# Loading the first dilated q and k in fp32 from SyncE, an earlier trigger for the casts of later batches, and shorter assumed latencies

## The chip, the cores and the metric

The kernel runs on one core of one Trainium2 chip. The metric is the device time of one execution in microseconds (us). Several executions of each kernel are timed, in rounds that alternate with runs of the kernel before on the same chip. A run counts as slow when it is over 1.5% above the fastest run of its own kernel; verdicts compare fast runs alone. A ratio is the mean time of one kernel's fast runs over that of the other's fast runs of the same rounds, so it is not quite the ratio of the medians quoted beside it. The interval in brackets is the 95% one.

In what follows PE is the TensorE, DVE the VectorE, ACT the ScalarE, POOL the GpSimd and SP the SyncE; "SPq" lines are SyncE's DMA issues. "L822" is a line of the kernel; lines of the changed kernel stand 10 or 11 below those of the kernel before (L811 there is L822 here).

## The reference, cut

```python
def attn(q, k, v):              # B, H, S, D = 8, 8, 576, 64
    scores = (1 / np.sqrt(D)) * np.matmul(q, k.transpose(0, 1, 3, 2))
    rel = pos[:, None] - pos[None, :]
    mask_plain = (rel >= 0) & (rel < 32)                        # heads 0 to 3
    mask_dil = (rel >= 0) & (rel < 128) & (rel % 4 == 0)        # heads 4 to 7
    ...                                                         # masked softmax
    return np.matmul(attn, v)

def moe(x, w_in, w_out, beta):  # x: 4608 tokens x 512, d_ff = 2048
    h = x @ w_in
    return (h * (1.0 / (1.0 + np.exp(-beta * h)))) @ w_out
```

All inputs are fp32. The output of the attention is `x`, token by token, for the feed-forward.

## The kernel before

The program isn't written in the order in which it runs. Every piece of work is an operation with its candidate engines, an assumed duration, the operations it depends on and a priority `vt`; a list scheduler simulates the engines and emits each instruction, to each engine's in-order stream, when the simulated engine is free. So an assumed latency changes no transfer. It changes where the instructions stand, and the hardware then keeps to that order.

The feed-forward runs in nine tiles of 512 tokens. A tile's 16 hidden blocks need `xT`, the transposed attention output. Batches 0 to 2 are loaded by GpSimd as a casting DMA and transposed by PE. From batch 3 on the way is longer:

```python
def back_dma(b, j, vt_of, vdone):            # attention output -> DRAM -> xT, for b >= 2, by SyncE
    ...                                      # spills of x; assumed: dma=1200, lat=2000
    o = plan.op([("SP", 1300)], lambda e: nc.sync.dma_start_transpose(out=cols, in_=rows[:]), out + dil,
                vt_of[f"X1{j}"], dma=1500, lat=3500)
...
def spread(e):                               # v of a batch into its padded place
    copy(e, vd[kv][:, :, :, 0:D], vd16_of[b])
o = plan.op([("POOL", 1100), ("DVE", 620)], spread, [ld["vd"][0], ...], vt, sbuf=True)
...
def t_pace(e, b=b, mid=mid):                 # what releases the casts of batch b >= 4
    nc.gpsimd.tensor_copy(out=pace[:], in_=xT[0:1, 0, mid - 1:mid + 1])
go = plan.op([("POOL", 150)], t_pace, behind + xready(mid - 1, mid + 1), b - 2.4)
for n, (z, h0) in enumerate(((0, 4), (1, 4), (0, 0), (1, 0))):
    c = cast(b, z, h0, [go], b - 2 + .01 * n)                 # GpSimd: fp32 -> bf16 scratch in DRAM
    ld[b]["x", z, h0] = crossbar(b, z, h0, [c] + ..., ...)    # SyncE: transposing load of the scratch
```

SyncE's one stream thus carries the transposes of k and q, the spills of x, the transposes of x and the stores of the output. A spill is the write of an attention output from the core's memory to DRAM.

The names in the traces: `dk` and `dq` are k and q of the dilated heads, `kT` and `qT` those of the plain heads; `pt` and `ptd` are the exponentials of the scores, plain and dilated; `vd` is v of the dilated heads; `g` is a hidden block after its gate; `s` is the scratch in DRAM that the casts write; `st` is a buffer for loads.

The softmax here doesn't subtract the row's maximum and nothing guards it: scores larger than these inputs give would overflow.

Of the kernel before, what the change touches and what calls it, by code (L numbers as in the profile page):

```python
# [174 lines left out]
def kernel(  # L175
# [55 lines left out]
    def copy(e, out, in_):  # L231
        (nc.scalar.copy if e == "ACT" else E[e].tensor_copy)(out=out, in_=in_)  # L232
# [12 lines left out]
    parity = const([P, 2], BF16, "parity")  # L245
    zero = const([P, 256], BF16, "zero")
    warm = const([P, 1], FP32, "warm")
    pace = const([1, 2], BF16, "pace")

    xT = const([P, NKT, B * S], BF16, "xT")  # L250
    g_t = [const([P, NFB, NTOK], BF16, f"g{i}") for i in range(2)]
# [129 lines left out]


    def dma(queue, out, in_):
        {"POOL": nc.gpsimd, "SP": nc.sync}[queue].dma_start(out=out, in_=in_)  # L384

    def load(queue, args, deps, vt, kb, rate=.4, issue=750, lat=1100):
        return plan.op(
# [3 lines left out]
    def direct_qk(b, z, h0, deps, vt):  # L391
        rows, n, dst = ((2 * GD, RD, std) if h0 else (P, RP, stp))
        src = bass.AP(tensor=(k, q)[z].tensor, offset=(k, q)[z][b, h0].offset,
                      ap=[[n * D, rows], [2 * S * D, 2], [1, n * D]])
        return load("POOL", (dst[z], src), deps, vt, 576, .41 if b else .33, lat=1100 if b else 1500)

    def plain_v(b, p0, c0):
        return bass.AP(tensor=v.tensor, offset=v[b, 0].offset + (p0 - WIN) * D + c0 * QT * D,
# [11 lines left out]
    def direct_vd(b, deps, vt, tdeps=()):  # L410
        src = v[b, 4:8].rearrange("h (t T) d -> t h (T d)", T=C)[0:P]
        out = [load("POOL", (vd16_of[b].rearrange("p h T d -> p h (T d)"), src), deps, vt, 512, .35)]
        for c in range(2):
            src = bass.AP(tensor=v.tensor, offset=v[b, 4].offset + ((P - WIN) * C + c) * D,
                          ap=[[2 * D, 2 * KTL], [S * D, 4], [1, D]])
            out.append(load("POOL", (vt_[b % 2][:, c, :, 0:D], src), list(tdeps), vt + (1.245 if b == 0 else .02 if b < DIRECT else 0) + .001 + .001 * c, 96, .2))
        return out

    scratch = {}
# [42 lines left out]
    def used(key, o):  # L462
        last.setdefault(key, []).append(o)
# [7 lines left out]
    def back_dma(b, j, vt_of, vdone):  # L471

        rows = dram_pool.tile([S // 2, HD], BF16, name=f"x{b}_{j}")
        out = [plan.op(
            [("SP", 500)], lambda e: nc.sync.dma_start(
                out=rows[:, 0:HD // 2].rearrange("(i m) c -> m i c", m=QT),
                in_=xsp[j][:].rearrange("p a x h d -> p a (x h d)")),
            [vdone[0, j], vdone[1, j]], vt_of[f"X1{j}"], dma=1200, lat=2000)]
        dep = [vdone[x, rp] for x in (2, 3) for rp in range(2)]
        t0, t1 = (0, S // 2 // C) if j == 0 else (S // 2 // C, P)  # L480
        right = rows[:, HD // 2:].rearrange("(t r) c -> t r c", r=C)
        dil = [plan.op(
            [("SP", 500)], lambda e: nc.sync.dma_start(
                out=right[0:t1 - t0], in_=xdm[t0:t1].rearrange("p r x h d -> p r (x h d)")),
            dep, vt_of["X2"] if j == 0 else vt_of["X11"], dma=1100, lat=2000)]
        if j:
            dil.append(plan.op(
                [("SP", 500)], lambda e: nc.sync.dma_start(
                    out=right[t1 - t0:].rearrange("u c e -> c u e"), in_=xdt[:].rearrange("p x h d -> p (x h d)")),
                [vdone["U"]], vt_of["X11"], dma=300, lat=2000))  # L490
        for x in range(2):
            wrote(("xs", x, j))
            for o in out:
                used(("xs", x, j), o)
        if j == 0:
            wrote("xdm", "xdt")
        for o in dil[:1]:
            used("xdm", o)
        for o in dil[1:]:
            used("xdt", o)  # L500
        cols = xT[:, :, b * S + j * S // 2:b * S + (j + 1) * S // 2]
        o = plan.op([("SP", 1300)], lambda e: nc.sync.dma_start_transpose(out=cols, in_=rows[:]), out + dil,
                    vt_of[f"X1{j}"], dma=1500, lat=3500)
        xcopy.append((range(NKT), b * S + j * S // 2, b * S + (j + 1) * S // 2, o))

    def attention(b, ld, names, vts):
# [4 lines left out]
        if b < DIRECT:  # L511
            for n in [x for x in names if x[0] in "KQ"]:
                z, kind, i = "KQ".index(n[0]), n[1], int(n[2])
                vt = vt_of[n]
                g = Group("a")
                src = ld["qk", z, 0 if kind == "P" else 4]
                tr = plan.op([("PE", (18 * mm(64) if kind == "P" else 6 * mm(QT)))],
                             lambda e, g=g, z=z, kind=kind, i=i: t_transposes(g, z, kind, i),
                             [src, ident], vt, acquire=g)
                used(("st", z), tr)  # L520
                def evac(e, g=g, z=z, kind=kind, i=i):
                    tp = bank(g, BF16)[:, 0:S]
                    if kind == "P":
                        dst = qT[kv][:, i] if z else kT[kv][:, i, WIN:]
                        copy(e, dst.rearrange("p (g j) -> p g j", j=RP), tp.rearrange("p (j g) -> p g j", j=RP))
                    else:
                        copy(e, (dk, dq)[z][kv][:, i].rearrange("p h (g s) -> p h g s", s=3),
                             tp.rearrange("p (s h g) -> p h g s", s=3, h=4))
                key = (("kT", "qT")[z], kv, i) if kind == "P" else (("dk", "dq")[z], kv, i)
                steps[n] = [plan.op([dve(S), act(S)], evac, [tr, fill1] + war(key), vt, group=g)]  # L530
                wrote(key)
        else:
            ready = {"D": [ld["x", 0, 4], ld["x", 1, 4]], "P": [ld["x", 0, 0], ld["x", 1, 0], fill1]}
# [262 lines left out]


    w_in_ld, w_out_ld = {}, {}
    gop, oread = {}, {}
    count = [0, 0]  # L800

    def slot_h(t, fb, c0, n, vt, apart):
# [37 lines left out]
    def block_cols(t, tb, vts, lo, hi, last_one):  # L840
        g = Group("z" if t == NTT - 1 else "o")
        prev = None
        for part in range(4):
            def mms(e, part=part):
                for fb in range(4 * part, 4 * part + 4):
                    nc.tensor.matmul(bank(g)[:, lo:hi], lhsT=g_t[t % 2][:, fb, tb * P:(tb + 1) * P],  # L846
                                     rhs=w_out_bf[:, fb, lo:hi], start=(fb == 0), stop=(fb == NFB - 1))
            deps = [prev] + [o for fb in range(4 * part, 4 * part + 4) for o in gop[t, fb]]
            prev = plan.op([("PE", 4 * mm(hi - lo))], mms, deps + [w_out_ld[part]], vts[part],
                           acquire=g if part == 0 else None, group=g)  # L850
        oread.setdefault(t, []).append(prev)
        ob = osb[count[1] % 4]
        key = ("osb", count[1] % 4)
        count[1] += 1
        r0 = t * NTOK + tb * P
        w = war(key)
        wrote(key)

        def evac(e):
            if e == "ACT":  # L860
                nc.scalar.mul(out=ob[:, lo:hi], in_=bank(g)[:, lo:hi], mul=0.5)  # L861
            else:
                nc.vector.tensor_single_scalar(out=ob[:, lo:hi], in_=bank(g)[:, lo:hi], scalar=0.5, op=ALU.mult)
        ev = plan.op([act(hi - lo), dve(hi - lo)], evac, [prev] + w, vts[3] - .01, group=g)
        so = plan.op([("ACT" if last_one and hi == HD else "SP", 400)],
                     lambda e: (nc.scalar if e == "ACT" else nc.sync).dma_start(out=out[r0:r0 + P, lo:hi], in_=ob[:, lo:hi]),
                     [ev], vts[3], dma=.5 * (hi - lo) * 1000 / 350)
        used(key, so)



    ld = {b: {} for b in range(B)}
    for n, (z, h0) in enumerate(((0, 4), (1, 4), (0, 0), (1, 0))):
        ld[0]["qk", z, h0] = direct_qk(0, z, h0, [], -9 + .01 * n)
    ld[0]["vd"] = direct_vd(0, [], -8.5, [fill3])
    ld[0]["vp"] = direct_vp(0, [fill3], -8.4)
    for n, (c0, c1) in enumerate(((0, 512), (512, 1024), (1024, 2048))):
# [21 lines left out]
    first = FIRST.split()  # L899
    names0 = first + ["zPRE", "zVAL"]  # L900
    vts = [-3 + 2 * i / len(first) for i in range(len(first))] + [-3, -2.5]
    vts[first.index("T"):len(first)] = [-.5, -.4, -.3, -.2]
    attention(0, ld[0], names0, vts)

    def xready(lo, hi, kts=range(NKT)):
# [2 lines left out]
    def loads(b):  # L908
# [7 lines left out]
            ld[b]["vp"] = direct_vp(b, war(("vp", b % 2)) + [fill4], base + .06)  # L916
            wrote(("vp", b % 2))
        else:
            behind = [ld[b - 1]["x", z, h0] for z in range(2) for h0 in (0, 4)] if b > DIRECT else []

            mid = (b - 2) * S + S // 2

            def t_pace(e, b=b, mid=mid):
                nc.gpsimd.tensor_copy(out=pace[:], in_=(  # L924
                    xT[0:1, 0, mid - 1:mid + 1] if b - 2 >= BY_DMA else g_t[b % 2][0:1, 0, 0:2]))
            go = plan.op([("POOL", 150)], t_pace, behind + (
                xready(mid - 1, mid + 1) if b - 2 >= BY_DMA else gop[b - 2, 0]), b - 2.4)
            for n, (z, h0) in enumerate(((0, 4), (1, 4), (0, 0), (1, 0))):
                c = cast(b, z, h0, [go], b - 2 + .01 * n)
                key = [(((("dk", "dq") if h0 else ("kT", "qT"))[z]), b % 2, i) for i in range(2)]  # L930
# [61 lines left out]
```

## Time and profile before

| | before |
|---|---|
| median of the runs beside the changed kernel | 305.85 us (305.43 to 306.01) |
| profiled span, granted clock | 304.8 us, 1.0 |
| PE busy | 295.4 us, 97% |
| PE waits over 0.25 us after 18 us | two: 0.26 (w_in) and 1.19 (dq) |

The prediction shows the lines for these. One view has to be added to it, the stream of SyncE (columns: start, length of the issue, what). It is that of the stretch which goes differently later:

```profile
81.77 2.70 SPq L502 DMA_TRANSPOSE xT<-x  x2
...
95.09 1.79 SPq L502 DMA_TRANSPOSE xT<-x  x1
97.07 4.55 SPq L438 DMA_TRANSPOSE dk<-s  x1
...
108.99 2.68 SPq L438 DMA_TRANSPOSE qT<-s  x1
```

The reader is to see the order: in 81 to 96 us three transposes of x, and only behind them the four transposes of batch 4's k and q, which wait for casts.

### The profile page before, as it was taken

How to read it: one execution, taken by the hardware profiler on the slowest of the kernel's cores; microseconds unless marked ns; L12 is line 12 of the kernel's file. 1: busy time of each engine (PE TensorE's matmuls, PEld its weight loads, DVE VectorE, ACT ScalarE, POOL GpSimd, SP SyncE). 2: the span in 40 equal slices, each digit the busy share in tenths (PEclk: the TensorE clock that was granted, in tenths of full speed). 3: DMA queues.
4: the chain of work that ended last, by engine and by line, in shares of the span. 5: the costliest groups of instructions: out<-in, count | busy, mean ns of one | idle time of the engine just before them, and what ended most of it. 6: DMA issues, size and time to landing. Idle time of an engine off the chain costs nothing.

```text
span 304.8 us, 6036 instructions
## 1 busy us (share of the span) xinstructions
PE 295.4 (97%) x2312; PEld 148.7 (49%) x2312; DVE 182.5 (60%) x422; ACT 171.0 (56%) x315; POOL 90.1 (30%) x132
## 2 busy tenths in 40 slices
PE   6899999999999989999999999999999999999995
PEld 5564545554544444444444444444444444444454
DVE  3468965888866745875677567757764434343300
ACT  2767963877547644755565556556554454554411
POOL 8978662746055104600470065100000000000000
PEclk9999999999999999999999999999999999999999
DMA  6999999999989998999699999992332100010122
GB/s 102 172 210 202 206 184 208 180 142 167 204 193 193 149 152 170 197 137 237 134 180 177 158 202 173 173 231 58 95 92 73 39 34 34 34 37 34 50 88 71
DMA packets 117376, 42.47 MB, mean 139 GB/s; under 512 B 93748, under 2 KB 110916, under 8 KB 117348
## 3 DMA queue, kind: packets, MB, share of 16 engines
q0 software_dynamic: 66672, 19.66, 64.9%
q1 hardware_dynamic: 50532, 22.36, 37.1%
q8 instruction: 18, 0.29, 0.4%
q14 instruction: 10, 0.08, 0.1%
q10 hardware_dynamic: 144, 0.07, 0.1%
HBM read 39.32 MB, written 18.87 MB: 191 GB/s over the span
## 4 chain that ended last, share of the span: by engine, by line
PE 74%; DMA 16%; POOL 3%; SPq 2%; DVE 2%; issue 1%; ACT 0%; POOLq 0%; DVEq 0%
PE bank L846 36%; PE bank L811 32%; DMA vd<-in_v_dram 4%; DMA st<-in_q_dram 4%; DMA dq<-s 3%; DMA w_in_bf<-in_moe_w_in_dram 3%; DMA x<-xsp 2%; DVE g L825 2%; SPq L438 2%; PE bank L673 1%; PE bank L729 1%; PE bank L639 1%; PE bank L714 1%; POOL st L384 1%; POOL vp L384 1%
## 5 line engine op out<-in xcount | busy, mean ns | idle before, releaser
L846 PE MATMUL bank<-w_out_bf,g 128*128 128x512 bf16 (+2 forms) x608 | 143.3, 368 | 0.0
L825 DVE SCALAR_TENSOR_TENSOR g<-tnh,bank 128x512 bf16<-128x512 bf16 x144 | 97.7, 685 | 74.4 <-ACT tnh L820 73.7
L811 PE MATMUL bank<-xT,w_in_bf 128*128 128x512 bf16 (+1 forms) x584 | 141.2, 376 | 0.3 <-DMA w_in_bf<-in_moe_w_in_dram 0.3
L820 ACT ACTIVATE tnh<-bank,beta_half 128x512 bf16<-128x512 f32 x144 | 98.5, 689 | 74.4 <-PE bank L811 73.3
L811 PEld LDWEIGHTS <-w_in_bf 128*128 128x128 bf16 x584 | 54.7, 98 | 60.4 <-DMA w_in_bf<-in_moe_w_in_dram 0.4
L846 PEld LDWEIGHTS <-g 128*128 128x128 bf16 x608 | 54.6, 98 | 55.7
L861 ACT ACTIVATE osb<-bank 128x512 f32<-128x512 f32 (+1 forms) x36 | 21.2, 589 | 32.0 <-PE bank L846 31.8
L576 ACT ACTIVATE pt<-bank 128x288 bf16<-128x288 f32 x64 | 21.5, 418 | 5.5 <-PE bank L673 5.4
L576 ACT ACTIVATE ptd<-bank 128x512 bf16<-128x512 f32 x32 | 16.9, 603 | 6.5 <-PE bank L639 6.5
L596 DVE TENSOR_TENSOR xsp<-bank,rcp 96x384 bf16<-96x384 f32 x32 | 17.7, 554 | 1.1
L384 POOL DMA_DIRECT2D vp<-in_v_dram x10 | 17.7, 1776 | 0.5 <-PE bank L455 0.5
L595 DVE RECIPROCAL rcp<-bank 128x4 f32<-128x4 f32 (+2 forms) x72 | 12.9, 180 | 6.3 <-PE bank L729 4.8
L580 DVE TENSOR_TENSOR ptd<-ptd,mask_d 128x512 bf16<-128x512 bf16 x27 | 11.9, 452 | 5.6 <-ACT ptd L576 4.5
L924 POOL COPY pace<-xT 1x2 bf16<-1x2 bf16 x4 | 0.8, 207 | 47.1 <-DMA xT<-x 37.1
L596 DVE TENSOR_TENSOR xdm<-bank,rcp 128x256 bf16<-128x256 f32 x32 | 13.6, 425 | 1.1
L384 POOL DMA_DIRECT2D vt<-in_v_dram x16 | 13.5, 1020 | 0.0
L384 POOL DMA_DIRECT2D s<-in_q_dram x10 | 13.5, 1347 | 0.0
L729 PEld LDWEIGHTS <-pt 128*128 128x128 bf16 x192 | 9.4, 97 | 5.9
L384 POOL DMA_DIRECT2D s<-in_k_dram x10 | 11.2, 1121 | 1.1 <-issue 1.1
L232 POOL COPY dkt<-dk 128x384 bf16<-128x384 bf16 x7 | 3.8, 544 | 22.8 <-DMA dk<-s 17.4
L729 PE MATMUL bank<-vp,pt 128*128 128x65 bf16 x192 | 10.4, 193 | 0.0
L714 PEld LDWEIGHTS <-ptd 128*128 128x128 bf16 x128 | 6.7, 98 | 4.7 <-issue 0.2
(108 smaller groups left out, 177.2 us busy)
## 6 DMA issues: line engine op xcount, KB each, us to landing
out_dram<-osb SPq DMA_DIRECT2D x35, 256.0 KB, 2.7
s<-in_k_dram POOLq DMA_DIRECT2D x10, 288.0 KB, 7.0
s<-in_q_dram POOLq DMA_DIRECT2D x10, 288.0 KB, 10.3
vp<-in_v_dram POOLq DMA_DIRECT2D x7, 384.0 KB, 18.2
w_out_bf<-in_moe_w_out_dram POOLq DMA_DIRECT2D x2, 1024.0 KB, 16.3
st<-in_k_dram POOLq DMA_DIRECT2D x6, 288.0 KB, 13.8
st<-in_q_dram POOLq DMA_DIRECT2D x6, 288.0 KB, 12.7
x<-xsp SPq DMA_DIRECT2D x12, 144.0 KB, 7.3
```

The costliest lines, as they stand in the source:

```text
L384: {"POOL": nc.gpsimd, "SP": nc.sync}[queue].dma_start(out=out, in_=in_)
L576: nc.scalar.activation(out=w(), in_=sc(), func=ACT.Exp, scale=SCALE)
L580: E[e].tensor_tensor(out=w(), in0=w(), in1=m(), op=ALU.mult)
L595: nc.vector.reciprocal(out=r, in_=p[..., D])
L596: nc.vector.tensor_tensor(out=dst, in0=p[..., 0:D], in1=r.unsqueeze(len(p.shape) - 1).to_broadcast(list(p.shape[:-1]) + [D]), op=ALU.mult)
L714: nc.tensor.matmul(pv[:, r, a], lhsT=ptd[:, x - 2, j, 2 * r + a], rhs=vd[kv][:, 2 * (x - 2) + a, 2 * r + j, 0:D + 1], start=True, stop=True)
L729: nc.tensor.matmul(pv[:, a, h2, :], lhsT=pt[x][:, (3 * j + a) * 2 + h2], rhs=vp[kv][:, (2 * x + h2) * NI + 3 * j + a, 0:D + 1], start=True ...
L811: nc.tensor.matmul(bank(g)[:, a:z], lhsT=w_in_bf[:, kt, fb * P:(fb + 1) * P], rhs=xT[:, kt, xo + a:xo + z], start=(i == 0 and kt == kts[0] ...
L820: nc.scalar.activation(out=th[:, 0:n], in_=bank(g)[:, 0:n], func=ACT.Tanh, scale=beta_half[:, fb:fb + 1])
L825: nc.vector.scalar_tensor_tensor(out=g_t[t % 2][:, fb, c0:c0 + n], in0=th[:, 0:n], scalar=1.0, in1=bank(g)[:, 0:n], op0=ALU.add, op1=ALU.mult)
L846: nc.tensor.matmul(bank(g)[:, lo:hi], lhsT=g_t[t % 2][:, fb, tb * P:(tb + 1) * P], rhs=w_out_bf[:, fb, lo:hi], start=(fb == 0), stop=(fb = ...
L861: nc.scalar.mul(out=ob[:, lo:hi], in_=bank(g)[:, lo:hi], mul=0.5)
```

## The change

The intent: start the first loads sooner by giving the dilated k and q of batch 0 to SyncE in fp32 (ACT and DVE then cast them); put the tail part of batch 0's attention into tile 0; release the casts of batch b at the first output block of tile b - 3, rather than when xT of batch b - 2 has landed; and tell the scheduler shorter latencies for the way of x back into xT. Cut to its core (left out: shorter assumed times for GpSimd's first loads, and bookkeeping):

```diff
+    def first_dil(z):
+        stage = g_t[1][...].bitcast(FP32)...
+        o = load("SP", (stage, src), [], -9.1 + .01 * z, 576, .41, 400, 300)
+        return [plan.op([("ACT", ...), ("DVE", ...)],
+                        lambda e, x=x: copy(e, std[z][:, x], stage[:, x]), [o], ...) for x in range(2)]
 ... spills of x
-            [vdone[0, j], vdone[1, j]], vt_of[f"X1{j}"], dma=1200, lat=2000)]
+            [vdone[0, j], vdone[1, j]], vt_of[f"X1{j}"], dma=900, lat=1300)]
 ... transpose of x
-                    vt_of[f"X1{j}"], dma=1500, lat=3500)
+                    vt_of[f"X1{j}"], dma=1400, lat=2200)
 ... batch 0
-        ld[0]["qk", z, h0] = direct_qk(0, z, h0, [], -9 + .01 * n)
+        ld[0]["qk", z, h0] = first_dil(z) if h0 else direct_qk(0, z, h0, [], -9 + .01 * n)
-    vts[first.index("T"):len(first)] = [-.5, -.4, -.3, -.2]
+    vts[first.index("T"):len(first)] = [.2,.35,.45,.5]
 ... trigger of the casts
-            behind = [ld[b - 1]["x", z, h0] for z in range(2) for h0 in (0, 4)] if b > DIRECT else []
-            go = plan.op([("POOL", 150)], t_pace, behind + xready(mid - 1, mid + 1) ..., b - 2.4)
+            ev, ob, key = evac_of[b - 3, 0] if b > DIRECT else (gop[b - 2, 0][-1], None, None)
+            go = plan.op([("POOL", 150)], t_pace, [ev], b - 2.4)       # copies one element of ob
```

More of the change, by code (lines that the diff above doesn't have):

```diff
@@ L247 @@
     warm = const([P, 1], FP32, "warm")
-    pace = const([1, 2], BF16, "pace")
+    pace = const([1, 1], FP32, "pace")
     xT = const([P, NKT, B * S], BF16, "xT")
@@ L383, in dma @@
     def dma(queue, out, in_):
-        {"POOL": nc.gpsimd, "SP": nc.sync}[queue].dma_start(out=out, in_=in_)
+        {"POOL": nc.gpsimd, "SP": nc.sync, "ACT": nc.scalar}[queue].dma_start(out=out, in_=in_)
     def load(queue, args, deps, vt, kb, rate=.4, issue=750, lat=1100):
@@ L394, in direct_qk @@
                       ap=[[n * D, rows], [2 * S * D, 2], [1, n * D]])
-        return load("POOL", (dst[z], src), deps, vt, 576, .41 if b else .33, lat=1100 if b else 1500)
+        return load("POOL", (dst[z], src), deps, vt, 576, .41, lat=1100 if b else 1300)
+    def first_dil(z):
+        stage = g_t[1][0:2 * GD, 8 * z:8 * z + 6, :].rearrange("p f n -> p (f n)").bitcast(FP32).rearrange(
+            "p (x e) -> p x e", x=2)
+        src = bass.AP(tensor=(k, q)[z].tensor, offset=(k, q)[z][0, 4].offset,
+                      ap=[[RD * D, 2 * GD], [2 * S * D, 2], [1, RD * D]])
+        o = load("SP", (stage, src), [], -9.1 + .01 * z, 576, .41, 400, 300)
+        return [plan.op([("ACT", 175 + .834 * RD * D), ("DVE", 160 + 1.042 * RD * D)],
+                        lambda e, x=x: copy(e, std[z][:, x], stage[:, x]), [o], -9.1 + .01 * z, sbuf=True) for x in range(2)]
     def plain_v(b, p0, c0):
@@ L415, in direct_vd @@
                           ap=[[2 * D, 2 * KTL], [S * D, 4], [1, D]])
-            out.append(load("POOL", (vt_[b % 2][:, c, :, 0:D], src), list(tdeps), vt + (1.245 if b == 0 else .02 if b < DIRECT else 0) + .001 + .001 * c, 96, .2))
+            out.append(load("POOL", (vt_[b % 2][:, c, :, 0:D], src), list(tdeps), vt + (1.255 if b == 0 else .02 if b < DIRECT else 0) + .001 + .001 * c, 96, .2))
         return out
@@ L484, in back_dma @@
                 out=right[0:t1 - t0], in_=xdm[t0:t1].rearrange("p r x h d -> p r (x h d)")),
-            dep, vt_of["X2"] if j == 0 else vt_of["X11"], dma=1100, lat=2000)]
+            dep, vt_of["X2"] if j == 0 else vt_of["X11"], dma=900, lat=1300)]
         if j:
@@ L489, in back_dma @@
                     out=right[t1 - t0:].rearrange("u c e -> c u e"), in_=xdt[:].rearrange("p x h d -> p (x h d)")),
-                [vdone["U"]], vt_of["X11"], dma=300, lat=2000))
+                [vdone["U"]], vt_of["X11"], dma=300, lat=1300))
         for x in range(2):
@@ L515, in attention @@
                 g = Group("a")
-                src = ld["qk", z, 0 if kind == "P" else 4]
+                srcs = ld["qk", z, 0 if kind == "P" else 4]
+                srcs = srcs if isinstance(srcs, list) else [srcs]
                 tr = plan.op([("PE", (18 * mm(64) if kind == "P" else 6 * mm(QT)))],
                              lambda e, g=g, z=z, kind=kind, i=i: t_transposes(g, z, kind, i),
-                             [src, ident], vt, acquire=g)
+                             srcs + [ident], vt, acquire=g)
                 used(("st", z), tr)
@@ L798 @@
     w_in_ld, w_out_ld = {}, {}
-    gop, oread = {}, {}
+    gop, oread, evac_of = {}, {}, {}
     count = [0, 0]
@@ L868, in block_cols @@
         used(key, so)
+        evac_of[t, tb] = ev, ob, key
     ld = {b: {} for b in range(B)}
     for n, (z, h0) in enumerate(((0, 4), (1, 4), (0, 0), (1, 0))):
-        ld[0]["qk", z, h0] = direct_qk(0, z, h0, [], -9 + .01 * n)
+        ld[0]["qk", z, h0] = first_dil(z) if h0 else direct_qk(0, z, h0, [], -9 + .01 * n)
     ld[0]["vd"] = direct_vd(0, [], -8.5, [fill3])
@@ L918, in loads, with t_pace @@
         else:
-            behind = [ld[b - 1]["x", z, h0] for z in range(2) for h0 in (0, 4)] if b > DIRECT else []
-            mid = (b - 2) * S + S // 2
-            def t_pace(e, b=b, mid=mid):
-                nc.gpsimd.tensor_copy(out=pace[:], in_=(
-                    xT[0:1, 0, mid - 1:mid + 1] if b - 2 >= BY_DMA else g_t[b % 2][0:1, 0, 0:2]))
-            go = plan.op([("POOL", 150)], t_pace, behind + (
-                xready(mid - 1, mid + 1) if b - 2 >= BY_DMA else gop[b - 2, 0]), b - 2.4)
+            ev, ob, key = evac_of[b - 3, 0] if b > DIRECT else (gop[b - 2, 0][-1], None, None)
+            def t_pace(e, b=b, ob=ob):
+                nc.gpsimd.tensor_copy(out=pace[:], in_=g_t[b % 2][0:1, 0, 0:1] if ob is None else ob[0:1, 0:1])
+            go = plan.op([("POOL", 150)], t_pace, [ev], b - 2.4)
+            if key:
+                used(key, go)
             for n, (z, h0) in enumerate(((0, 4), (1, 4), (0, 0), (1, 0))):
```

## The prediction

> **What bounds the kernel now.** I read the page first, then stretches of busy time, then the PE timeline with the idle time before each piece, then the chain that ended last, then the POOL and SyncE timelines.
>
> The page and the stretches (columns: stretch, its length, then busy time and count for PE, PEld, DVE, ACT, POOL, then granted clock, DMA share, GB/s):
>
> ```profile
> PE 295.4 (97%) x2312; PEld 148.7 (49%) x2312; DVE 182.5 (60%) x422; ACT 171.0 (56%) x315; POOL 90.1 (30%) x132
> ...
> 0.00:5.00 5.00, 3.87 (x22) 2.85 (x22) 2.19 (x17) 1.49 (x2) 3.77 (x11) 1.00 0.42 58
> ...
> 20.00:25.00 5.00, 5.00 (x38) 3.18 (x36) 2.84 (x7) 3.73 (x8) 3.39 (x7) 1.00 1.25 205
> ...
> 100.00:120.00 20.00, 18.72 (x145) 9.18 (x144) 12.66 (x33) 10.03 (x19) 3.26 (x6) 1.00 1.37 163
> ...
> 200.00:220.00 20.00, 20.00 (x151) 9.79 (x150) 14.11 (x34) 12.19 (x22) 0.00 (x0) 1.00 0.56 125
> ```
>
> PE is busy 295.4 of 304.8 us at full clock. After 20 us it is full in nearly every stretch; 100 to 120 us is the only one that misses over 0.5 us. So there is little to win: the idle 9.4 us, plus the warm-up matmuls on a zero tile, which count as busy but do nothing. Where they are:
>
> ```profile
> 1.13 4.06 PE L958 MATMUL bank<-zero 128*128 128x256 bf16 x22 [1.13 <-DVE warm L290]
> 6.05 0.68 PE L448 MATMUL bank<-ident_b,st 96*128 96x96 bf16 x12 [0.87 <-DMA st<-in_k_dram]
> ...
> 11.76 0.75 PE L455 MATMUL bank<-ident_b,st 64*64 64x64 bf16 x36 [0.63 <-DMA st<-in_q_dram]
> ...
> 19.18 1.04 PE L811 MATMUL bank<-xT,w_in_bf 128*128 128x512 bf16 x4 [0.26 <-DMA w_in_bf<-in_moe_w_in_dram]
> ...
> 110.72 0.62 PE L639 MATMUL bank<-dq,dk 64*128 64x128 bf16 x16 [1.19 <-DMA dq<-s]
> ```
>
> The head (to 19.18 us, the first feed-forward matmul) waits for loads: dilated k at 6.05, plain q at 11.76, the first third of w_in at 19.18. Later one wait stands out: 1.19 us for dq of batch 4 at 110.72. The chain says the same:
>
> ```profile
> 10.80 8.33 DMA w_in_bf<-in_moe_w_in_dram
> ...
> 27.17 12.28 DMA vd<-in_v_dram
> ...
> 45.05 12.21 DMA st<-in_q_dram
> ...
> 101.67 8.92 DMA dq<-s
> ```
>
> The load stream runs near PE up to about 57 us. And what triggers batch 4's casts, whose product that dq is:
>
> ```profile
> 82.50 0.60 ACT L861 ACTIVATE osb<-bank 128x512 f32<-128x512 f32 x1 [1.95 <-PE bank L846]
> ...
> 86.99 0.18 POOL L924 COPY pace<-xT 1x2 bf16<-1x2 bf16 x1 [10.97 <-DMA xT<-x]
> 87.48 0.61 POOL L384 DMA_DIRECT2D s<-in_k_dram  x1 [0.31 <-issue]
> ```
>
> The casts go out at 87.5 us, after xT of batch 2 has landed, though the first output block of tile 1 (the first line) was evacuated 4 us before.
>
> **What the Trainium skill says.** "DMA: Bandwidth & Descriptors", section "SWDGE vs HWDGE vs iDMA": a DMA that casts must be issued by GpSimd, so moving these loads to SyncE forces fp32 staging and a cast on a compute engine. Its section "Latency and other measured facts" gives about 0.6 us to the first byte from SyncE and about 1 us from GpSimd. The trace agrees in direction: the SyncE load of beta, issued at 0.81, moves its bytes between about 1.8 and 2.1 us; GpSimd's first load, issued at 1.36, moves none before 2.5. The section "Issuing engines are not separate DMA queues" says that all run on the same 16 engines and interleave; so the second queue starts earlier but adds no bandwidth. "SBUF — State Buffer" warns that a VectorE fp32 copy within SBUF can lock GpSimd out of writing descriptors; no run here shows that yet.
>
> **The change part by part.**
>
> Dilated k and q by SyncE. GpSimd loses two issues, 0.79 + 0.65 = 1.44 us, less a few gaps: every later issue moves up some 1.35 us (w_in from 10.80 to about 9.45). SyncE starts at 0.81, so bytes flow from about 1.8 instead of 2.5 us. Bytes read are unchanged; bytes written double for these two. Does that cost? The casting stream writes 205 to 215 GB/s of bf16, so it reads about 420; an output store, fp32 on both sides, peaks at 389 GB/s in the trace. The limit is therefore about 400 GB/s on the fp32 side, the two loads (1.18 MB) take 3 us in either form, and the fp32 form costs nothing extra. The old stream also ramped slowly (31, 65, 114, 157 GB/s in the half-microseconds from 2.5 to 4.5), worth about 1.1 us of full rate. So the stream as a whole moves up by 0.7 to 1.75 us, and w_in with it: 19.1 to 17.4 to 18.2.
>
> The price is four casts of 96x768. ScalarE copies 576 in 0.64 us and 288 in 0.40, so 0.83 ns an element, 768 in 0.80; VectorE at most 0.95. Two run side by side for k, two for q, while both engines are idle (ScalarE is idle 4.21 us before its first copy at 6.52). Dilated k lands at about 3.7 and is cast by 4.6; PE, with 18 warm-up matmuls rather than 22, starts near 4.7 rather than 6.05. Dilated q shares the engines with plain k, lands near 5.8, is cast by 6.7, and its scores can start near 8.3 rather than 9.1. Plain q, 11.76 before, comes near 9.5. From there ScalarE (4.46 of 5 us busy from 10 to 15) and VectorE (4.58 of 5 from 15 to 20) set the pace of the attention chain, so it moves up by what its start moves, about 1 us, plus part of the 0.6 us wait for plain q. Sum for the head: -1.4 us. The order of PE agrees in size: 26 warm-up matmuls instead of 35, 9 x 0.16 = 1.4 us.
>
> Tail of batch 0 within tile 0: the same matmuls at nearly the same places (its values move behind the transposes of batch 1's k). PE work is unchanged; 0 us.
>
> Casts behind the first output block of tile b - 3: for batch 4 that block is evacuated at 82.50 + 0.60 = 83.1, and in the new order PE gets there about 1.5 us sooner plus the head's gain, so the casts go out near 80.5 instead of 87.5. In SyncE's order batch 4's transposes now also stand before xT of batch 3, not behind. dq lands several us earlier; its 1.19 us wait goes: -1.2 us. Batches 5 to 7 gain 2 to 3 us of slack that nothing waits for.
>
> The shorter assumed latencies change no duration, only PE's order: the first hidden block of tile 2 stands about 4.8 us of PE work earlier, the last values of batch 2 only 1.5 earlier. Before, xT of batch 2 was in by 86.9 and wanted at 91.06: 4.1 us to spare. 4.1 - 4.8 + 1.5 leaves about 0.8 us, and the earlier casts now share the DMA engines with that very transfer. Tile 3 is tight in the same way. I charge +0.6 us for this.
>
> Sum: -1.4 - 1.2 + 0.6 = -2.0 us, so about 303.7 us.
>
> **Rivals.** (a) The new trigger only moves the wait: xT of batch 2 or 3 lands late and PE stands 1 to 3 us at the start of tile 2 or 3. For it: the 0.8 us above, and that a spill of x issued at 88.18 beside the casts took 6.87 us while others took about 3.5. Against: DMA share is only 0.6 to 1.0 from 82 to 90 us. Time: 305 to 306. (b) The head's gain is hidden: PE starts early but overtakes the load stream and waits for batch 1's dilated k, which now stands two feed-forward groups sooner in PE's order. For it: the loads on the chain up to 57 us. Time: about 304.5. (c) The head gains more than its start, because plain q no longer interrupts ScalarE and slow ramp and issue gaps both vanish: -2.5 us. Time: 302.5. (d) VectorE's fp32 copies block GpSimd's descriptors and w_in is late: under 1 us, as there are two of under 1 us each.
>
> **Range and chances.** All the idle and warm-up time that could go is about 1.4 + 1.2 + 2 us; 2% is 6.1 us, so faster by over 2% would need more than there is: 0.02. Slower by over 2% needs 6 us of new waits: 0.02. Within 2%: 0.96. The middle is 303.7, the range from rival (c) with nothing lost, 302.1, to rival (a), 305.6.
>
> **What would show it.** Right: first feed-forward matmul near 17.8; no wait for dq near 110; the casts of batch 4 near 80.5; PE busy about 1.4 us less. Wrong: a PE wait for xT at the start of tile 2 (near 86) or 3 (near 112), for st of batch 1 near 25, or w_in landing at 19 as before because fp32 writes do cost engine time.

## The result, and the profile after

| | before | after |
|---|---|---|
| median | 305.85 us (4 runs) | 316.97 us (313.71 to 321.8; 4 runs, one of them slow) |
| ratio of the fast runs | 1 | 1.033 [1.0243, 1.0417] |
| granted clock of the runs | 1.0 | 1.0, 0.984, 0.978 (the slow one), 0.999 |
| profiled span | 304.8 us | 312.0 us (the fastest run, 313.71, clock 1.0) |

The kernel became 3.3% slower. The profiled execution happens to be the best of the four, so it shows 7.2 us of the loss.

First the timeline of PE after, with the idle time before each piece in brackets:

```profile
7.19 1.14 PE L458 MATMUL bank<-ident_b,st 96*128 96x96 bf16 x12 [2.04 <-ACT st L232]
...
22.04 4.87 PE L822 MATMUL bank<-xT,w_in_bf 128*128 128x512 bf16 x28
...
108.98 0.62 PE L650 MATMUL bank<-dq,dk 64*128 64x128 bf16 x16
...
114.92 4.54 PE L822 MATMUL bank<-xT,w_in_bf 128*128 128x512 bf16 x19 [1.28 <-DMA xT<-x]
...
178.29 2.76 PE L822 MATMUL bank<-xT,w_in_bf 128*128 128x512 bf16 x12 [1.73 <-DMA xT<-x]
...
198.44 0.98 PE L740 MATMUL bank<-vp,pt 128*128 128x65 bf16 x12 [1.67 <-DVE pt L591]
...
213.17 2.76 PE L822 MATMUL bank<-xT,w_in_bf 128*128 128x512 bf16 x12 [1.62 <-DMA xT<-x]
```

The first transposes now begin at 7.19 (6.05 before), and the first long hidden run at 22.04. In the timeline before it was

```profile
20.81 4.88 PE L811 MATMUL bank<-xT,w_in_bf 128*128 128x512 bf16 x28
```

the same 28 matmuls, so the head lost 1.2 us. The wait for dq is gone (the line at 108.98 has no bracket): 1.2 us won. In their place stand three waits for xT and one for pt: 1.28 + 1.73 + 1.67 + 1.62 = 6.3 us, and a small one of 0.29 at 163.45. The sum, 1.2 - 1.2 + 6.6 = 6.6, accounts for all but 0.6 of the 7.2 us.

GpSimd's stream shows the new trigger at work, 4 us earlier than the 87.48 of before (the prediction's estimate was 80.5):

```profile
83.29 0.18 POOL L934 COPY pace<-osb 1x1 f32<-1x1 f32 x1 [8.24 <-ACT osb L872]
83.53 0.61 POOL L384 DMA_DIRECT2D s<-in_k_dram  x1
```

And SyncE's stream shows what xT is behind now:

```profile
80.95 2.68 SPq L512 DMA_TRANSPOSE xT<-x  x2
...
89.62 2.33 SPq L448 DMA_TRANSPOSE dk<-s  x1
92.05 4.92 SPq L448 DMA_TRANSPOSE dq<-s  x1
97.08 2.72 SPq L448 DMA_TRANSPOSE kT<-s  x1
99.89 1.23 SPq L485 DMA_DIRECT2D x<-xsp  x1
104.39 1.29 SPq L448 DMA_TRANSPOSE qT<-s  x1
...
107.92 5.49 SPq L512 DMA_TRANSPOSE xT<-x  x2
```

No transpose of x stands between 83.6 and 107.9 us any more. The transpose of plain q cannot start before its cast has landed, and everything written behind it on SyncE waits with it. The chain that ended last says so in a row (start, length, what):

```profile
87.88 16.49 DMA s<-in_q_dram
104.39 1.29 SPq L448
106.40 4.61 DMA x<-xsp
111.02 3.76 DMA xT<-x
114.92 4.11 PE bank L822 x18
```

The cast of plain q (16.49 us in flight) releases SyncE's transpose at 104.39, then come a spill and the transpose of x, and PE starts tile 3 when that lands. The chain repeats the pattern at 154.59 and 188.20 for tiles 5 and 6, there without a spill.

The wait for pt at 198.44 has another cause. DVE's stream:

```profile
197.75 0.43 DVE L232 COPY vd<-st 128x1024 bf16<-128x1024 bf16 x1 [3.39 <-DMA st<-in_v_dram]
198.09 0.96 DVE L591 TENSOR_TENSOR pt<-pt,maskn_PP 128x288 bf16<-128x288 bf16 x4
```

The spread of v into vd is on DVE here (that of batch 7; from batch 3 on the changed kernel has two of them there, the kernel before one). It waits 3.39 us for its load, with four masks behind it that were ready.

### The profile page after: what moved, and what is told of

It reads as the page before. It is cut to its first block, busy times and chain, and to the rows that moved or that the text cites. A ratio compares the mean times of both kernels' runs of the same rounds, so it can differ in the third digit from the quotient of the medians.

```text
span 312.0 us, 5988 instructions
## 1 busy us (share of the span) xinstructions
PE 294.9 (95%) x2266; PEld 149.4 (48%) x2303; DVE 185.4 (59%) x433; ACT 171.2 (55%) x312; POOL 85.5 (27%) x126
## 4 chain that ended last, share of the span: by engine, by line
PE 63%; DMA 24%; POOL 4%; SPq 2%; ACT 2%; issue 2%; DVE 1%; ACTq 0%; POOLq 0%
PE bank L822 29%; PE bank L857 27%; DMA s<-in_q_dram 15%; DMA xT<-x 5%; DMA g<-in_q_dram 2%; DMA x<-xsp 1%; POOL s L384 1%; SPq L448 1%; POOL vt L384 1%; PE bank L465 1%; PE bank L458 1%; PE bank L684 1%; PE bank L740 1%; PE bank L650 1%; ACT ptd L587 1%
## 5 line engine op out<-in xcount | busy, mean ns | idle before, releaser
L857 PE MATMUL bank<-w_out_bf,g 128*128 128x512 bf16 (+2 forms) x587 | 140.3, 367 | 2.0 <-issue 0.8
L934 POOL COPY pace<-osb 1x1 f32<-1x1 f32 x4 | 0.7, 178 | 53.1 <-ACT osb L872 53.1
L232 POOL COPY dkt<-dk 128x384 bf16<-128x384 bf16 x5 | 2.7, 542 | 24.9 <-DMA dk<-s 11.2
```

Source lines behind the costliest of these rows:

```text
L857: nc.tensor.matmul(bank(g)[:, lo:hi], lhsT=g_t[t % 2][:, fb, tb * P:(tb + 1) * P], rhs=w_out_bf[:, fb, lo:hi], start=(fb == 0), stop=(fb = ...
```

## The experiments

Theory A came in stages; the records below carry it as it stood when each group was submitted. The rivals that matter are named there.

### One part at a time: e1, e2, e3

e1 is the kernel before with the SyncE loads and the moved tail alone; e2 with the shorter assumed latencies alone; e3 with the new trigger alone, through the schedule. The diffs are the corresponding parts of the change.

> The kernel before with the SyncE loads of dilated k and q alone (and the moved tail of batch 0). If the head costs what the trace of the changed kernel shows (first long run of hidden matmuls at 22.04 instead of 20.81 us), this runs about 1.2 to 1.8 us over the kernel before (307 to 307.7), with its wait for dq near 110 us kept and no PE wait for xT over 1 us. If the forecast's head was right after all and the 1.2 us came from something else, about 304.4.

> The kernel before with the shorter assumed latencies of the way back to xT alone; only the order of instructions moves. Theory A (the order asks for xT too soon): the hidden blocks of tiles 5 and 6 now stand 9.6 us of PE work behind the last values instead of 14.8 and 13.5, PE waits for xT there, 309 to 311. Theory B (the new trigger of the casts is what makes xT late, the order is innocent): 305 to 306.5.

> The kernel before with the new trigger of the casts alone. Theory A: dq of batch 4 comes in time, its 1.2 us wait goes, 304.3 to 305.3. Theory B: PE waits for xT at tiles 3, 5 or 6, 309 or more.

| | median | ratio | profiled span |
|---|---|---|---|
| e1, head alone | 307.64 us | 1.0068 [1.0012, 1.0125] | 305.6 |
| e2, latencies alone | 311.58 us | 1.0187 [1.0136, 1.0238] | 308.8 |
| e3, trigger alone | 311.17 us | 1.0172 [1.0105, 1.0239] | 310.8 |

The before of that call: 306.51 us. None of the three parts wins anything by itself. The head costs 0.7% where it should have won. In e1's profile the wait for dq, which was expected to stay, is replaced by one of 1.12 us for g at 110.07. In e2 PE waits 1.93 us for xT at 144.42, 0.94 at 176.23, and 2.81 us at 108.33 for a gate g. DVE shows why g is late; again something stands ahead of it that waits:

```profile
107.32 0.36 DVE L232 COPY dkt<-dk 128x384 bf16<-128x384 bf16 x1 [4.62 <-DMA dk<-s]
107.60 1.28 DVE L825 SCALAR_TENSOR_TENSOR g<-tnh,bank 128x512 bf16<-128x512 bf16 x2
```

In e3 the longest waits are for xT: 1.79 us at 91.79 and 2.79 at 122.31 (then 0.75 for xT and 0.79 for pt). The first of them isn't due to SyncE's order, which up to the transposes of batch 2 is that of before. The chains show the second of these two transposes in flight, in e2, whose casts go out only later, at 86.46, and in e3, whose casts go out at 82.18:

```profile
82.19 3.66 DMA xT<-x
```

```profile
82.37 9.29 DMA xT<-x
```

### Head and trigger together, old latencies: e4

The changed kernel with the four assumed latencies of before put back.

> The changed kernel with the old assumed latencies (the head and the new trigger stay). Theory A: most of the 7 to 11 us goes; head +1.3, dq -1.2, about 306, and granted clock 1.0 in every run. Theory B: stays near the changed kernel, 312 or more.

320.35 us (316.06 to 321.52, two of the four slow), ratio 1.0386 [1.0299, 1.0473]. This was the first miss that mattered. Theory A, then "the shortened latencies are the cause", fell: with the old ones the kernel is as slow as with the new. Its profile has one wait of 5.00 us, for a gate at 102.67, behind a spread of v on DVE that waits 5.64 us for its load. And PE, with 9 warm-up matmuls fewer than before, is busy for 300.3 us rather than 295.4: after the wait the granted clock is lower, 0.71 in 100 to 104 us, 0.50 in 104 to 108, 0.94 in 108 to 112.

### The trigger in an unchanged order: e5

Only what the pace copy reads is changed; the scheduler is still given the old dependency, so that every instruction on every engine keeps the place it had before.

```diff
-                nc.gpsimd.tensor_copy(out=pace[:], in_=xT[0:1, 0, mid - 1:mid + 1] ...)
+                nc.gpsimd.tensor_copy(out=pace[:], in_=ob[0:1, 0:1] ...)
             go = plan.op([("POOL", 150)], t_pace, behind + xready(mid - 1, mid + 1) ..., b - 2.4)
```

> The kernel before, every instruction in its old place on every engine; only what the pacing copy reads is changed (first output block of tile b - 3 instead of xT of batch b - 2), so the casts of batches 4 to 7 go out 2 to 5 us sooner. If sooner casts themselves delay xT by sharing the DMA engines: xT of batch 2 lands near 91 instead of 86.9 us, PE waits 0 to 2 us for it near 91, the wait for dq near 110 shrinks, 305.5 to 308. If the trigger only harms through the order that it makes the schedule take: no wait for xT, the wait for dq goes, 304.5 to 305.5.

304.77 us, ratio 0.9981 [0.993, 1.0031], profiled span 302.7. The timeline of PE has no wait over 0.25 us after 18 us; at the two critical places:

```profile
90.34 10.52 PE L811 MATMUL bank<-xT,w_in_bf 128*128 128x512 bf16 x47
...
108.75 0.62 PE L639 MATMUL bank<-dq,dk 64*128 64x128 bf16 x16
```

So the earlier casts and their traffic do no harm where they fall in e5: xT of batch 2 is there by 90.34, and dq no longer waits. Its transposes of x are issued from 80.25 on and the casts from 82.68, 2.43 us behind; in e3 the casts are only 1.23 us behind (80.95 and 82.18). What costs in e3 is what follows from the order into which the scheduler puts things when it is told of the new trigger, and a part of that is traffic: the casts meet the transposes of x in flight.

### The spreads of v off DVE: e6 and e7

```diff
-        o = plan.op([("POOL", 1100), ("DVE", 620)], spread,
+        o = plan.op([("POOL", 1100)] if b >= DIRECT else [("POOL", 1100), ("DVE", 620)], spread,
```

e6 is the changed kernel with this, e7 is e4 with this.

> The changed kernel with the copy of v into vd (batches 3 to 7) held on GpSimd; two of these had moved to VectorE, whose queue then stood still for a load. If that is a cause of its own: the wait of 1.7 us near 198 us and the 0.3 near 163 go, 2 us faster than the changed kernel on one profile (about 310 in its span), the three waits for xT stay. If it only moves the wait: no change.

> The run with head and trigger but old latencies (320 us), with the copy of v into vd held on GpSimd. Its wait of 5.0 us near 102 us stood behind such a copy on VectorE, and the granted clock fell to 0.5 for the 4 us after it. If the copy is the cause: that wait and the low clock both go, 5 to 9 us faster, 311 to 315. If PE would have waited there for something else anyway: 318 to 320.

e7: 312.3 us, ratio 1.0227 [1.0179, 1.0275], against e4's 1.0386: the 5.00 us wait is gone, and with it about 0.016 x 306 = 5 us of the fast runs. 2.73 us for xT at 121.74 and 1.34 for g at 173.84 remain in its profile. e6: 319.83 us, ratio 1.0426 [1.035, 1.0503], no better than the changed kernel. Its waits for pt are gone, but those for xT grew to 4.66, 2.57 and 2.89 us, the first of them at tile 2:

```profile
93.60 8.49 PE L822 MATMUL bank<-xT,w_in_bf 128*128 128x512 bf16 x32 [4.66 <-DMA xT<-x]
```

There SyncE issued the two transposes from 83.35 on, the casts followed at 84.30, and PE asked at 93.60 - 4.66 = 88.94. The second of them, from its own issue on:

```profile
84.77 8.70 DMA xT<-x
```

The scheduler assumed 1.3 + 0.9 + 1.4 + 2.2 = 5.8 us from the start of one issue to its landing (0.9 is what it adds to every transfer for its start).

### More warm-up in the head: e8

e1 with the SyncE loads assumed 1000 ns later, so that the scheduler fills the gap with more warm-up matmuls.

```diff
-        o = load("SP", (stage, src), [], -9.1 + .01 * z, 576, .41, 400, 300)
+        o = load("SP", (stage, src), [], -9.1 + .01 * z, 576, .41, 400, 1300)
```

> Head change alone with the SyncE loads assumed 1 us later, so that the schedule puts 3 more warm-up matmuls into the wait for dilated k. Its first transposes took 1.14 instead of 0.68 us after 2 us of idle PE. If that cold PE is what the head loses: half a us to 1 us faster than the head alone, 306.5 to 307. If the late landing of dilated q (8.67 instead of 7.47 us) is what it loses: 307 to 308, no gain.

306.48 us, ratio 1.0028 [0.9999, 1.0057], against 1.0068 for e1. The intervals overlap, so this settles only that the head's loss is small either way. In its profile the granted clock is 0.58, 0.50, 0.50 and 0.71 in the four stretches of 2 us from 8 us on, so the extra warm-up didn't keep the clock up, and a cold PE isn't ruled out as a part of the head's loss.

### The true latencies: e9, e10, and e12

e9 is the changed kernel, all parts in, with two edits: the spreads on GpSimd as in e6, and latencies near those that the traces show. e10 is the same without the changed head. e12 is the changed kernel with the latencies alone.

```diff
-            [vdone[0, j], vdone[1, j]], vt_of[f"X1{j}"], dma=900, lat=1300)]       (three spills)
+            [vdone[0, j], vdone[1, j]], vt_of[f"X1{j}"], dma=900, lat=2500)]
-                    vt_of[f"X1{j}"], dma=1400, lat=2200)
+                    vt_of[f"X1{j}"], dma=1400, lat=6000)
```

> The changed kernel with all its parts, but the schedule is told how long the loads back of x really take (2500 for a spill of x and 6000 for its transpose in place of 1300 and 2200), and the spread of v into vd stays on GpSimd from batch 3 on. In its order of PE the distance from the last values of batch t to the first hidden block of tile t is 16.6, 25.7, 13.9, 13.9, 13.9 us for tiles 2 to 6 (after: 11.1, 12.7, 11.4, 12.4, 12.4). Theory A (what costs is the order, which lets PE ask for xT before it can be there, and the copies of v ahead of the gates on VectorE; both then lower the clock): waits for xT and for pt above 1 us are gone, what remains is the head's loss of 1 to 1.5 us less the 1.2 us for dq: 305 to 308. Rival B (the changed head alone drags the clock and the load stream behind it, whatever comes later): 309 or more, without long waits but with a clock below 0.98. Rival C (casts and transposes on SyncE ahead of xT delay it without limit, a longer distance is eaten up): xT waits of 1 us and more remain, 310 or more.

> The same without the changed head: the kernel before, the new trigger through the schedule, the true latencies and the spread of v on GpSimd. Theory A: 304 to 306, no PE wait above 0.5 us after 20 us, clock 1.0, so 1 us or more below the run with the head. Rival B: also about 305, but then far (4 us or more) below the run with the head. Rival C: 309 or more.

> One factor against the changed kernel: nothing but the four assumed latencies (spills of x 2500 in place of 1300, transpose of x 6000 in place of 2200). The distances from last values to first hidden block are those of the run with the true latencies (16.6, 25.7, 13.9, 13.9, 13.9 us); of the five spreads of v on VectorE only one of batches 3 to 7 is left there, that of batch 4 or 5. Theory A (order alone): 305 to 308, at most one wait above 1 us after 20 us, that one behind the spread of v. If the assumed latencies are not enough and the place of the spreads of v carries most of the loss: 310 or more.

e9: 306.19 us, ratio 1.0006 [0.9985, 1.0026]; its three fast runs are 305.62 to 306.56. e10: 306.36 us, ratio 1.0005 [0.9981, 1.0029]. Rival B falls, as e9 with the head is as fast as e10 without it. Rival C falls for the fast runs, by their time. e10 isn't quite what theory A expected: it is not below e9, and PE waits 0.64 us for xT at 94.39 and 1.55 for g at 109.07, where DVE held a copy of q that waited for dq. One of e9's four runs, the profiled one, is slow (312.0 us): PE waits 2.56 us for xT at 121.81 there, and 1.91 at 77.88 for a pt masked on GpSimd, and the clock is 0.77 and 0.80 in the two stretches of 4 us from 120. So the distance, though longer, is still short at times, and the profile of a fast run of e9 is missing.

e12: 313.98 us, ratio 1.0291 [1.0254, 1.0327], over the 305 to 308 that theory A expected. The waits for xT are gone, as it said, but one spread of v left on DVE is enough. DVE's and PE's timelines of e12:

```profile
102.11 0.43 DVE L232 COPY vd<-st 128x1024 bf16<-128x1024 bf16 x1 [8.75 <-DMA st<-in_v_dram]
102.46 1.88 DVE L836 SCALAR_TENSOR_TENSOR g<-tnh,bank 128x512 bf16<-128x512 bf16 x3
```

```profile
103.19 12.95 PE L822 MATMUL bank<-xT,w_in_bf 128*128 128x512 bf16 x52 [5.88 <-DVE g L836]
```

and the stretches around it (length, busy time and count of PE, PEld, DVE, ACT and POOL, granted clock, DMA share, GB/s):

```profile
96.00:100.00 4.00, 1.31 (x7) 0.49 (x5) 0.00 (x0) 1.65 (x3) 0.00 (x0) 0.95 1.48 124
100.00:104.00 4.00, 0.81 (x3) 0.25 (x3) 1.89 (x4) 0.00 (x0) 0.54 (x1) 0.50 1.60 170
104.00:108.00 4.00, 4.00 (x15) 1.57 (x14) 1.62 (x3) 1.83 (x3) 0.58 (x2) 0.70 1.87 160
108.00:112.00 4.00, 4.00 (x20) 1.86 (x19) 3.12 (x6) 3.12 (x6) 0.00 (x0) 1.00 1.45 234
```

The wait costs twice: PE stands for 5.88 us, and then does 15 matmuls in the 4 us from 104 where the stretch from 108, at full clock, has 20.

Four kernels form a square, in which only the two edits vary (median, ratio):

| | spread of v may go to DVE | spread of v on GpSimd (b of 3 and more) |
|---|---|---|
| short assumed latencies | changed kernel: 316.97, 1.033 | e6: 319.83, 1.0426 |
| long assumed latencies | e12: 313.98, 1.0291 | e9: 306.19, 1.0006 |

Either edit alone leaves the loss, both together remove it from the fast runs. Each of the two faults hides behind the other. Each edit also moves other instructions; the timelines name the waits, but no run moves one instruction alone.

### The head's loads by themselves: e11

e1, with every casting load of GpSimd held until the four casts of the SyncE loads are done.

```diff
-        ... else direct_qk(0, z, h0, [], -9 + .01 * n)
+        ... else direct_qk(0, z, h0, ld[0]["qk", 0, 4] + ld[0]["qk", 1, 4], -9 + .01 * n)
     (the same dependency on the loads of v, w_in and w_out)
```

> The head alone, but every casting load of GpSimd is held until the four casts are done, so that SyncE's loads of dilated k and q have the engines to themselves. The kernel is slower by several us by construction; what is read is when k and q land. If they land late in the changed kernel (6.3 and 8.7 us) because they share the engines with GpSimd's plain k and q, k now lands at 3.5 to 4.5 and q at 5 to 6. If the fp32 form from one queue is itself slow (240 to 320 GB/s were seen), k lands at 5 or later and q at 6.5 or later.

One run, 309.87 us, slower by construction. The chain of e11 has the load of k, and GpSimd's stream shows that its first load came after it:

```profile
0.81 5.30 DMA g<-in_k_dram
```

```profile
7.28 0.87 POOL L384 DMA_DIRECT2D st<-in_k_dram  x1
```

k still lands at 6.11 us (6.3 in the changed kernel), so its late landing isn't due to GpSimd's loads. q is there no later than 8.02, where ACT begins its cast, and the view of the stretches has its last bytes before 7.5:

```profile
6.50:7.50 1.00, 0.48 (x10) 0.48 (x11) 0.19 (x1) 0.48 (x2) 1.00 (x5) 0.92 0.37 108
7.50:8.50 1.00, 1.00 (x10) 0.55 (x7) 0.54 (x1) 1.00 (x2) 1.00 (x2) 0.50 0.00 0
```

In the changed kernel q landed at 8.7, so 0.7 to 1.2 us of its lateness goes when GpSimd's loads are held. From 2.5 to 6.5 us the same view has 261, 267, 230 and 226 GB/s with nothing but these two loads and the 8 KB of beta under way. That SyncE's two loads, issued 0.46 us apart, share the engines and so land late together is likely, but no run here loads k alone.

## Why the prediction was wrong

The prediction was 303.7 us, in a range to 305.6, with a chance of 0.02 for slower by over 2%. It came to 316.97, and to 313.71 in the best run. What failed above all is the price of the new order: the prediction charged +0.6 us for it, under the assumed latencies, and nothing under the casts. By its own steps:

**Head, -1.4 us: wrong in sign, and small.** The failed step is the arrival of the SyncE loads, "the two loads (1.18 MB) take 3 us in either form, and the fp32 form costs nothing extra", from which k was to land at about 3.7 and q near 5.8. They landed at 6.3 and 8.7. The rate was 226 to 267 GB/s even without other loads (e11), where the prediction used 400, a rate taken from a casting stream in full flow and from a store. k came no earlier than GpSimd had brought it, q 1.2 us later (at least half of that for GpSimd's loads beside it, by e11), and the casts came on top. The trace shows the first long hidden run 1.2 us later; e1 shows 1.0068. That w_in would no longer be the limit was right. The first twelve transposes took 1.14 us, against 0.68 before, and the first two matmuls that add the dilated mask 1.01 against 0.60, at a recorded clock of 1.00. e8 has 1.14 and 1.03 us for such work at 9.92 and 12.58, where the clock recorded is 0.50. So PE in the changed head may have run at about half its clock as well; the record says otherwise, and this stays open. Of rival (d) a trace is seen, but not in w_in: a GpSimd memset of 16x16 that took 0.10 us before took 0.52 from 8.86 on, ending just after VectorE's fp32 cast of 8.70 to 9.33, and w_in was issued at 9.59, as forecast. ("The first third of w_in" is by the sizes a quarter, 512 of 2048 KB.)

**Tail of batch 0, 0 us: not tested by itself.** It is part of e1, which leaves room for little.

**Casts and the wait for dq, -1.2 us: right in the wait, wrong in the sum.** The wait went (108.98 in the changed kernel; 108.75 in e5). The casts went out at 83.5 rather than 80.5; the head's gain on which that relied didn't come. But the term has no price for the order that comes with the trigger: alone and through the schedule it made the kernel slower, 1.0172 (e3), and in the old order it did not, 0.9981 (e5).

**Shorter assumed latencies, +0.6 us: the term that was mis-sized most.** The mechanism, xT asked for before it lands, is rival (a), and it was seen; its size and its reach were not. Alone the shorter latencies cost 1.0187 (e2), about 0.0187 x 306 = 5.7 us. The prediction worked out tile 2's slack as 0.8 us and charged 0.6 for all tiles. But "tile 3 is tight in the same way" was a sentence and not a sum. In the profiled run tile 2 doesn't wait, and tiles 3, 5 and 6 wait 4.6 us in all. For the same reason the range ended where it did: rival (a) was given "1 to 3 us", once.

**What was read the wrong way round.** The prediction saw that "in SyncE's order batch 4's transposes now also stand before xT of batch 3, not behind", and counted it as a gain for dq. The chain after shows it as the loss: the transpose of q waits for a cast 16.49 us in flight, and the spill and transpose of x stand behind it in the same stream.

**What was missing altogether.** The prediction never asked where the instructions of DVE went. A copy that may run on either engine moved in front of the gates and masks, and waited there for its load: 1.67 us of PE's time in the changed kernel, 5.88 in e12, 5.00 in e4. It also took a PE wait to cost its own length. After the long ones the granted clock fell to half for some us; in e4 that is part of a rise of PE's busy time to 300.3 us.

**Order or traffic.** The argument that DMA share was only 0.6 to 1.0 where the casts would go was about traffic. It holds in e5, which has the casts early in the old order and loses nothing, and fails where the casts come about 1 us behind the transposes of x: these then took 9.29 (e3) and 8.70 us (e6) against 3.66 without casts (e2). So traffic lengthens the way of x; the order decides whether the two meet, and whether PE asks in the meantime. How much of the loss is due to each wasn't separated. e9 has all parts of the change in another order, and comes out level with the kernel before: the two gains that were sought aren't there, or cancel against the head.

**Open.** The three timed runs of the changed kernel that weren't profiled were 2 to 8 us slower than the profiled one, one of them at a clock of 0.999; which waits they had isn't known. No version here beats the kernel before by more than its spread: e5, the best, is at 0.9981 with an interval that holds 1.

## What to carry to other kernels

When a scheduler lays out in-order streams, an assumed latency or a dependency is a decision on order. Compare the streams of every engine, that of the DMA-issuing one too, and ask of each instruction that waits for a transfer what stands behind it. Keep copies that wait for a load off an engine whose other work feeds the critical one, and tell the scheduler the latency under load (8.70 and 9.29 us here for one transpose of x), not the best one seen (3.66). When an experiment that mends one cause changes nothing, try it together with the other cause before dropping it.

## What the Trainium skill lacked or had wrong

- "DMA: Bandwidth & Descriptors", section "Issuing engine by pattern", calls the SyncE path generally faster. Bytes did flow earlier (80 GB/s in 1.5 to 2.5 us against 8 before), but k of 576 KB landed about 5.5 us after its issue from SyncE in fp32, and about 4.7 us after it from GpSimd with the cast (issued 1.36, there at 6.05). The two forms write 576 and 288 KB, so this doesn't compare the issuing engines alone. The page has no figure for a load of this size from SyncE; e11 shows 226 to 267 GB/s.
- None of the pages used here speaks of the cost of order on one issuing engine: a transpose on SyncE that waited for its cast held back the spill and transpose of x behind it, and PE waited 4.6 us in all for xT in the changed kernel.
- None of the pages used here has a time for a transposing load beside other traffic: one transpose of x took 3.66 us without casts (e2), and 9.29 (e3) and 8.70 (e6) with casts issued about 1 us after the first transpose of the pair.
- "TensorE: Matmul & The Clock Gate", Part 1, says that the clock halves after at least one idle window of about 3.4 us. The runs agree for long waits: 0.50 after 5.00 us (e4) and after 5.88 us (e12), while waits of 1.28 to 1.73 us left it at 1.00 (the changed kernel). Shorter waits than the window were sometimes enough: one of 2.56 us was followed by 0.77 and 0.80 over 8 us in the slow run of e9, and one of 2.41 us, before the first transposes at 7.02, by 0.50 in 7.5 to 8.5 us in e11. One of 2.89 us in e6 (at 220.72) left the clock at 1.00.
